# The high half of the first MoE's gated product moves to ScalarE, and the low half of its last two groups to VectorE

## The chip, the cores and the metric

The kernel runs on one core of one Trainium2 chip. The metric is the device time of one execution in microseconds (us): the median of several runs. A profile of one execution shows every engine: TensorE (PE, with its weight loads as PEld), VectorE (DVE), ScalarE (ACT), GpSimd (POOL) and the queue of SyncE that issues the DMAs (SP).

## The reference

Three stages are chained: an attention with a decaying mask, a first MoE layer with a maximum of three products, and a second one with a rational function. Shapes: 4 batches of 576 tokens, 8 heads of 64, so 2304 tokens by 512; 768 and 2048 hidden columns.

```python
scores = scale * q @ k.T + decay            # causal, decay from cumsum(log(clip(f)))
attn = softmax(scores);  x = attn @ v       # 2304 x 512

h = np.maximum(np.maximum(x @ w1, x @ w2), x @ w3)     # 2304 x 768
x = h @ w_out                                          # 2304 x 512

h = x @ w_in                                           # 2304 x 2048
P = a[0] + a[1]*h + a[2]*h*h + a[3]*h*h*h
Q = 1.0 + abs(b[0])*abs(h) + abs(b[1])*h*h
out = (P / (Q + 1e-6)) @ w_out2                        # 2304 x 512
```

The weights arrive as 64-bit floats, which the kernel converts itself.

## The kernel before

**Numbers in two parts.** Matmul operands are float32r. A value is written as a high part (the value rounded to float32r by a copy) and a low part (the value less the high one), and each product is three matmuls: high by high, high by low, low by high.

**Groups and units.** Tokens go in groups (batch b, part g): g = 0 has 320 columns, g = 1 has 256, so there are eight groups. For each group the first MoE has 18 units `moe1_h` (six column blocks fc, three matrices j) and then four units `moe1_o` (dc).

- `moe1_h` (lines 422 to 442) makes 12 matmuls into one PSUM bank (lines 429 to 431). For j = 0 ScalarE copies the bank into an SBUF tile `m` (line 434); for j = 1 and 2 VectorE takes the maximum of that and the next bank (line 436). After j = 2 the gated product is split into the tile `hh`: its high part on line 440 (GpSimd multiplies by one), its low part on line 441 (GpSimd subtracts).
- `moe1_o` (lines 444 to 459) runs over all six `hh` of the group: three matmuls for each fc, on lines 453 and 454 (by the high part) and 455 (by the low part), into `x2p`. ScalarE and VectorE split the result into `xo` (lines 457 and 458), and a DMA takes it to DRAM.

**What runs beside it.** The units are put between the steps of the attention. Its normalisation of `e` (line 360) and copies of keys and queries (lines 267 and 281) are on GpSimd, its exponentials (line 350) and copies of transposed weights `pt` (line 385) on ScalarE. The last two groups (b = 3) are left over and come after the attention: from there `tail["n"]` is a number and no longer None, `hbank` hands out banks of three pools, and the units stand between 32 conversions of the second MoE's input weights (`convert_wi`, which calls `convert`, lines 151 to 170). One conversion is: a load, ScalarE's absolute value (line 160), VectorE's four operations 161, 162, 163 and 166 on 128 x 256 values, ScalarE's copy to the high part `wih` (line 169), GpSimd's subtraction to the low part `wil` (line 170). Three tiles `cv_wi` go round.

**Who sets the order.** Each engine works through its own queue in order. The order in a queue is not that of the code: a scheduler takes the recorded operations and lays them out by an estimate of its own of when each can run. So a changed operation moves others. Only the second MoE from its second tile on (`manual_schedule`) stands as written.

Of the kernel before, what the change touches and what calls it, by code (L numbers as in the profile page):

```python
# [11 lines left out]
AF = mybir.ActivationFunctionType  # L12
ALU = mybir.AluOpType
# [21 lines left out]
def kernel(  # L35
    ctx: ExitStack, tc: tile.TileContext, q, k, v, f, w1, w2, w3, w_out, m2_in, m2_out, m2_a, m2_b, out
):
    nc = tc.nc
# [11 lines left out]
    def r32(ap):  # L50
        return ap.bitcast(F32)
# [361 lines left out]
    tail = {"n": None}  # L413

    def hbank(name):
        pool, tag = ps_h, "h"
        if tail["n"] is not None:
            pool, tag = TAILP[tail["n"] % len(TAILP)]
            tail["n"] += 1
        return pool.tile([P, 512], F32, name=name, tag=tag)  # L420

    def moe1_h(b, g, fc, j):
        w = GQ[g][1] - GQ[g][0]
        nm_ = f"{b}_{g}_{fc}"
        xs = [xt[b, dc, g] for dc in range(NDC)]
        wh, wl = w1t[fc]
        hp_ = hbank(f"h{j}_{nm_}")
        for dc in reversed(range(NDC)):
            nc.tensor.matmul(hp_[:, :w], wh[:, j, dc], xs[dc][:, 1], start=(dc == NDC - 1), stop=False)  # L429
            nc.tensor.matmul(hp_[:, :w], wh[:, j, dc], xs[dc][:, 0], start=False, stop=False)  # L430
            nc.tensor.matmul(hp_[:, :w], wl[:, j, dc], xs[dc][:, 0], start=False, stop=(dc == 0))  # L431
        nxt = mpool.tile([P, 320], F32, name=f"m{j}_{nm_}", tag="mx", bufs=3)
        if j == 0:
            nc.scalar.activation(nxt[:, :w], hp_[:, :w], AF.Copy)
        else:
            nc.vector.tensor_tensor(nxt[:, :w], cur[0][:, :w], hp_[:, :w], op=ALU.max)  # L436
        cur[0] = nxt
        if j == 2:
            hh = mpool.tile([P, 2, 320], F32R, name=f"hh_{nm_}", tag="hh", bufs=6)
            nc.gpsimd.tensor_scalar(hh[:, 0, :w], nxt[:, :w], 1.0, 0.0, op0=ALU.mult, op1=ALU.add)  # L440
            nc.gpsimd.tensor_tensor(hh[:, 1, :w], nxt[:, :w], r32(hh[:, 0, :w]), op=ALU.subtract)
            hs[b, g, fc] = hh

    def moe1_o(b, g, dc):
# [16 lines left out]
    def moe1_units(b, g):  # L461
        return [lambda fc=fc, j=j: moe1_h(b, g, fc, j) for fc in range(NF1) for j in range(3)] + [
            lambda dc=dc: moe1_o(b, g, dc) for dc in range(NDC)
        ]
# [72 lines left out]
    for step in range(len(slots) + 2):  # L537
# [4 lines left out]
        if u is not None and u.pair.n + 1 < len(pairs):  # L542
            n = u.pair.n + 1
# [252 lines left out]
```

## Time and profile before

| | |
|---|---|
| median of 3 runs | 1014.16 us (1014.15 to 1014.49) |
| the profiled execution's own time | 1014.65 us |
| its span, first to last instruction | 1012.8 us |
| TensorE busy | 984.6 us, 97% of the span |
| VectorE, ScalarE, GpSimd busy | 74%, 61%, 28% |
| mean granted TensorE clock | 0.989 |

The span is 1.85 us shorter than the profiled execution's time, and that time is 0.49 us over the median. The attention with the first six groups lasts to about 520 us, the last two groups of the first MoE from there to 607.5 us, the second MoE to the end. The busy time of TensorE includes the ends of pipelined matmuls, which are modelled: a matmul of 320 columns is shown as 0.31 us, while the next one starts 0.15 us after it. A granted clock of 1.00 is 2.4 GHz, of 0.50 it is 1.2 GHz; a value between is a stretch with both.

### The profile page before, as it was taken

What the parts mean: (1) busy time and instruction counts of PE and PEld (TensorE: products, weight loads), DVE (VectorE), ACT (ScalarE), POOL (GpSimd) and SP (SyncE); (2) the same over time, 40 slices, a digit from 0 to 9 for tenths busy, and PEclk for the clock granted to TensorE, in tenths of its full rate; (3) what the DMA queues carried; (4) which work ended last, traced back from release to release, by engine and by line L of the source; (5) the groups of instructions that cost most, each with busy time, mean ns of one, the idle gap of its engine ahead of it and who ended that gap; (6) DMA issues with size and microseconds to landing.
All of it is one profiled execution on the core that took longest, in us unless ns stands there. A gap on an engine that the chain in (4) does not pass through costs nothing.

```text
span 1012.8 us, 16900 instructions
## 1 busy us (share of the span) xinstructions
PE 984.6 (97%) x5780; PEld 831.2 (82%) x5780; DVE 750.6 (74%) x1744; ACT 613.5 (61%) x1409; POOL 286.7 (28%) x498
## 2 busy tenths in 40 slices
PE   8989999999999999999998989999999999999998
PEld 5657778887888888988898987888888888899997
DVE  4779984555677676644349676988988888899997
ACT  4775665656655566554434336766766666677775
POOL 1545763543554554443326440000000000000000
PEclk9998999999999999999999999999999999999999
DMA  4574223213444355221034529301001100200000
GB/s 122 162 213 132 79 57 89 47 41 104 119 128 151 104 154 179 81 59 48 1 116 146 177 80 344 128 1 49 35 1 63 42 1 1 95 10 1 32 1 32
DMA packets 118453, 86.69 MB, mean 86 GB/s; under 512 B 67280, under 2 KB 103136, under 8 KB 118368
## 3 DMA queue, kind: packets, MB, share of 16 engines
q1 hardware_dynamic: 118368, 85.62, 27.9%
q8 instruction: 46, 0.75, 0.3%
q14 instruction: 39, 0.32, 0.1%
HBM read 62.90 MB, written 22.69 MB: 85 GB/s over the span
## 4 chain that ended last, share of the span: by engine, by line
PE 77%; DVE 14%; issue 3%; DMA 3%; ACT 2%; POOL 1%; SPq 0%; DVEq 0%; POOLq 0%; ACTq 0%
PE oo L719 7%; PE oo L720 7%; PE oo L718 6%; PE o L399 6%; PE hq L669 6%; PE hq L671 6%; PE hq L670 6%; PE tp L381 5%; PE h L429 5%; PE h L430 4%; PE h L431 4%; PE s L342 2%; PE x2p L453 2%; PE x2p L455 2%; PE x2p L454 2%
## 5 line engine op out<-in xcount | busy, mean ns | idle before, releaser
L429 PE MATMUL h<-x,w1h 128*128 128x320 f32 (+1 forms) x576 | 176.9, 307 | 2.1 <-DVE m L436 2.0
L430 PE MATMUL h<-x,w1h 128*128 128x320 f32 (+1 forms) x576 | 173.0, 300 | 0.0
L431 PE MATMUL h<-x,w1l 128*128 128x320 f32 (+1 forms) x576 | 172.7, 300 | 0.0
L360 POOL TENSOR_SCALAR e<-e,rs 64x64 f32<-64x64 f32 (+4 forms) x160 | 88.6, 565 | 114.5 <-DVE rs L356 87.9
L350 ACT ACTIVATE e<-e,st 64x64 f32<-64x64 f32 (+4 forms) x160 | 89.3, 558 | 51.7 <-DVE st L344 48.9
L429 PEld LDWEIGHTS h<-x,w1h 128*128 128x128 f32 x576 | 110.3, 192 | 8.8 <-DVE m L436 3.7
L719 PE MATMUL oo<-wp,gh 128*128 128x512 f32 x288 | 112.8, 392 | 0.0
L718 PE MATMUL oo<-wp,gh 128*128 128x512 f32 x288 | 112.4, 390 | 0.0
L430 PEld LDWEIGHTS h<-x,w1h 128*128 128x128 f32 x576 | 110.2, 191 | 2.2 <-issue 2.0
L344 DVE CUSTOM_DVE_ANT_0 e<-s,mask 128x320 f32<-128x320 f32 (+3 forms) x160 | 68.1, 432 | 57.6 <-PE s L343 37.3
L431 PEld LDWEIGHTS h<-x,w1l 128*128 128x128 f32 x576 | 110.0, 191 | 0.1
L720 PE MATMUL oo<-wp,gl 128*128 128x512 f32 x288 | 108.8, 392 | 0.0
L678 ACT ACTIVATE s<-hq 128x512 f32<-128x512 f32 (+1 forms) x80 | 44.3, 554 | 97.2 <-PE hq L671 97.1
L385 ACT ACTIVATE pt<-tp 128x384 f32<-128x384 f32 (+3 forms) x160 | 69.8, 471 | 31.6 <-PE tp L381 28.7
L399 PE MATMUL o<-pt,v 128*64 128x256 f32 (+3 forms) x512 | 83.0, 371 | 0.3 <-ACT pt L385 0.3
L381 PE MATMUL tp<-ident,e 128*128 128x128 f32 (+2 forms) x480 | 81.4, 278 | 0.6 <-POOL e L360 0.5
L681 DVE SCALAR_TENSOR_TENSOR s<-s,ab,u 128x512 f32<-128x512 f32 (+1 forms) x80 | 55.8, 698 | 31.8 <-ACT u L679 31.6
L671 PE MATMUL hq<-x,wil 128*128 128x512 f32 (+1 forms) x192 | 70.4, 366 | 0.0
L669 PE MATMUL hq<-x,wih 128*128 128x512 f32 (+1 forms) x192 | 70.4, 366 | 0.0
L670 PE MATMUL hq<-x,wih 128*128 128x512 f32 (+1 forms) x192 | 70.3, 366 | 0.0
L453 PE MATMUL x2p<-hh,wo 128*128 128x320 f32 (+1 forms) x192 | 59.6, 314 | 7.2 <-POOL hh L440 5.9
L381 PEld LDWEIGHTS tp<-ident,e 128*128 128x128 f32 (+2 forms) x480 | 54.3, 132 | 13.6 <-issue 7.0
(128 smaller groups left out, 2444.6 us busy)
## 6 DMA issues: line engine op xcount, KB each, us to landing
raw_w<-in_moe_w_dram SPq DMA_DIRECT2D x18, 512.0 KB
raw_wp<-in_moe_w_out_dram SPq DMA_DIRECT2D x32, 256.0 KB
wpd<-wp SPq DMA_DIRECT2D x32, 256.0 KB
raw_wi<-in_moe_w_in_dram SPq DMA_DIRECT2D x32, 256.0 KB
wp<-wpd SPq DMA_DIRECT2D x10, 768.0 KB
x2d<-xo SPq DMA_DIRECT2D x16, 320.0 KB
out_dram<-ob SPq DMA_DIRECT2D x18, 256.0 KB
kn<-in_k_dram SPq DMA_DIRECT2D x32, 128.0 KB
```

Source lines behind the costliest of these rows:

```text
L350: nc.scalar.activation(e[:nr], e[:nr], AF.Exp, bias=m, scale=-1.0, accum_out=l)
L381: nc.tensor.transpose(tp[:kr, dst : dst + nr], self.e[i][:nr, Q0[c] : Q1[c]], ident[:nr, :nr])
L399: nc.tensor.matmul(ot[SIDES[i][0], q0 - lo : w], p.v[:kr, c, i], p.pt[g][:kr, i, col : col + hi - q0], start=(j == 0), stop=(j == len(orde ...
L429: nc.tensor.matmul(hp_[:, :w], wh[:, j, dc], xs[dc][:, 1], start=(dc == NDC - 1), stop=False)
L430: nc.tensor.matmul(hp_[:, :w], wh[:, j, dc], xs[dc][:, 0], start=False, stop=False)
L431: nc.tensor.matmul(hp_[:, :w], wl[:, j, dc], xs[dc][:, 0], start=False, stop=(dc == 0))
L669: nc.tensor.matmul(hp_[:, :w], wih[:, dc, fs], xh, start=(dc == 0), stop=False)
L670: nc.tensor.matmul(hp_[:, :w], wih[:, dc, fs], xl, start=False, stop=False)
L671: nc.tensor.matmul(hp_[:, :w], wil[:, dc, fs], xh, start=False, stop=(dc == NDC - 1))
L718: nc.tensor.matmul(o, g[0][:, ts_], wh_, start=(fc == 0), stop=False)
L719: nc.tensor.matmul(o, g[0][:, ts_], wl_, start=False, stop=False)
L720: nc.tensor.matmul(o, g[1][:, ts_], wh_, start=False, stop=(fc == NF2 - 1))
```

## The change

The high part of `hh` is written by ScalarE as a copy, in all 48 places. The low part stays on GpSimd in the 36 that are recorded during the attention, and goes to VectorE in the 12 of the last two groups. Nothing else is edited; from line 441 on the changed kernel's line numbers are one higher, so its low part is line 442 and the split of `xo` lines 458 and 459.

```diff
         if j == 2:
             hh = mpool.tile([P, 2, 320], F32R, name=f"hh_{nm_}", tag="hh", bufs=6)
-            nc.gpsimd.tensor_scalar(hh[:, 0, :w], nxt[:, :w], 1.0, 0.0, op0=ALU.mult, op1=ALU.add)
-            nc.gpsimd.tensor_tensor(hh[:, 1, :w], nxt[:, :w], r32(hh[:, 0, :w]), op=ALU.subtract)
+            nc.scalar.activation(hh[:, 0, :w], nxt[:, :w], AF.Copy)
+            eng = nc.gpsimd if tail["n"] is None else nc.vector
+            eng.tensor_tensor(hh[:, 1, :w], nxt[:, :w], r32(hh[:, 0, :w]), op=ALU.subtract)
             hs[b, g, fc] = hh
```

The scheduler lays the queues out anew. In the rows below a name such as `hh_3_0_4` is the tile of batch 3, part 0, block fc 4; `m1` and `m2` are the maxima after j = 1 and j = 2; `cv_wi_2_7` is the tile of one conversion.

**VectorE, the last two groups, around block 4 of group (3, 0).** Before:

```order
L161 TENSOR_SCALAR cv_wi_2_7_7317<-cv_wi_2_7_7317 128x256
L166 SCALAR_TENSOR_TENSOR cv_wi_0_7_7284<-raw_wi_0_7_7201,cv_wi_0_7_7284 128x256
L162 TENSOR_SCALAR cv_wi_2_7_7317<-cv_wi_2_7_7317 128x256
L161 TENSOR_SCALAR cv_wi_0_8_7327<-cv_wi_0_8_7327 128x256
L436 TENSOR_TENSOR m2_3_0_4_7116<-m1_3_0_4_7081,h2_3_0_4_7103 128x320
L163 SCALAR_TENSOR_TENSOR cv_wi_2_7_7317<-raw_wi_2_7_7229,cv_wi_2_7_7317 128x256
L162 TENSOR_SCALAR cv_wi_0_8_7327<-cv_wi_0_8_7327 128x256
L166 SCALAR_TENSOR_TENSOR cv_wi_2_7_7317<-raw_wi_2_7_7229,cv_wi_2_7_7317 128x256
L163 SCALAR_TENSOR_TENSOR cv_wi_0_8_7327<-raw_wi_0_8_7239,cv_wi_0_8_7327 128x256
L166 SCALAR_TENSOR_TENSOR cv_wi_0_8_7327<-raw_wi_0_8_7239,cv_wi_0_8_7327 128x256
L436 TENSOR_TENSOR m1_3_0_5_7189<-m0_3_0_5_7154,h1_3_0_5_7176 128x320
L436 TENSOR_TENSOR m2_3_0_5_7224<-m1_3_0_5_7189,h2_3_0_5_7211 128x320
```

And of the change:

```order
L161 TENSOR_SCALAR cv_wi_2_7_7317<-cv_wi_2_7_7317 128x256
L166 SCALAR_TENSOR_TENSOR cv_wi_0_7_7284<-raw_wi_0_7_7201,cv_wi_0_7_7284 128x256
L436 TENSOR_TENSOR m2_3_0_4_7116<-m1_3_0_4_7081,h2_3_0_4_7103 128x320
L162 TENSOR_SCALAR cv_wi_2_7_7317<-cv_wi_2_7_7317 128x256
L161 TENSOR_SCALAR cv_wi_0_8_7327<-cv_wi_0_8_7327 128x256
L163 SCALAR_TENSOR_TENSOR cv_wi_2_7_7317<-raw_wi_2_7_7229,cv_wi_2_7_7317 128x256
L162 TENSOR_SCALAR cv_wi_0_8_7327<-cv_wi_0_8_7327 128x256
L442 TENSOR_TENSOR hh_3_0_4_7118<-m2_3_0_4_7116,hh_3_0_4_7118 128x320
L166 SCALAR_TENSOR_TENSOR cv_wi_2_7_7317<-raw_wi_2_7_7229,cv_wi_2_7_7317 128x256
L163 SCALAR_TENSOR_TENSOR cv_wi_0_8_7327<-raw_wi_0_8_7239,cv_wi_0_8_7327 128x256
L166 SCALAR_TENSOR_TENSOR cv_wi_0_8_7327<-raw_wi_0_8_7239,cv_wi_0_8_7327 128x256
L436 TENSOR_TENSOR m1_3_0_5_7189<-m0_3_0_5_7154,h1_3_0_5_7176 128x320
```

The maximum `m2_3_0_4` stands two conversion operations earlier, and the low part of `hh_3_0_4` four operations behind it. Block 4 of group (3, 1) has the same pattern, with its maximum one operation (an L166) earlier and its low part two operations behind it. Each of the other ten blocks has one L442 more in this queue.

**ScalarE at the same place.** Before:

```order
L160 ACTIVATE cv_wi_0_8_7327<-raw_wi_0_8_7239 128x256
L169 ACTIVATE wih_7013<-cv_wi_0_7_7284 128x2x128
L434 ACTIVATE m0_3_0_5_7154<-h0_3_0_5_7141 128x320
L169 ACTIVATE wih_7013<-cv_wi_2_7_7317 128x2x128
L169 ACTIVATE wih_7013<-cv_wi_0_8_7327 128x2x128
```

And of the change:

```order
L160 ACTIVATE cv_wi_0_8_7327<-raw_wi_0_8_7239 128x256
L169 ACTIVATE wih_7013<-cv_wi_0_7_7284 128x2x128
L440 ACTIVATE hh_3_0_4_7118<-m2_3_0_4_7116 128x320
L434 ACTIVATE m0_3_0_5_7154<-h0_3_0_5_7141 128x320
L169 ACTIVATE wih_7013<-cv_wi_2_7_7317 128x2x128
L169 ACTIVATE wih_7013<-cv_wi_0_8_7327 128x2x128
L440 ACTIVATE hh_3_0_5_7226<-m2_3_0_5_7224 128x320
```

What stands ahead of the high part, the copy `wih` of `cv_wi_0_7`, waits for an L166 that is ahead of `m2_3_0_4` on VectorE too.

**ScalarE during the attention, around block 3 of group (2, 0), of the change.**

```order
L385 ACTIVATE pt_16_0_1_5426<-tp1_16_1_1_5546 128x384
L385 ACTIVATE pt_16_0_1_5426<-tp2_16_1_1_5551 64x256
L169 ACTIVATE wp_15_1_5641<-cv_wp_15_1_5642 128x256
L440 ACTIVATE hh_2_0_3_5666<-m2_2_0_3_5664 128x320
L350 ACTIVATE e1_17_1_0_5683,rs_17_1_0_5675<-e1_17_1_0_5683,st_17_1_0_5674 128x192
L350 ACTIVATE e2_17_1_0_5689,rs_17_1_0_5675<-e2_17_1_0_5689,st_17_1_0_5674 128x320
```

Here the high part, which waits for a maximum of VectorE, stands ahead of two exponentials; before, GpSimd had it, between a conversion (L170) and the low part, with three normalisations (L360) behind.

## Rows read from the trace of the kernel before

**Rows 1.** The page, busy time of each engine over the span.
```profile
PE 984.6 (97%) x5780; PEld 831.2 (82%) x5780; DVE 750.6 (74%) x1744; ACT 613.5 (61%) x1409; POOL 286.7 (28%) x498
```
**Rows 2.** Stretches: start:end, length, busy us of each engine, granted clock, DMA share, GB/s.
```profile
557.30:561.00 3.70, 3.70 (x17) 3.70 (x17) 1.72 (x3) 0.42 (x1) 2.57 (x4) 0.55 0.00 0
...
598.60:602.10 3.50, 3.24 (x15) 2.94 (x15) 0.73 (x2) 0.42 (x1) 2.35 (x4) 0.51 0.00 0
...
625.00:1012.80 387.80, 383.79 (x1756) 324.69 (x1754) 342.07 (x557) 266.43 (x475) 0.00 (x0) 1.00 0.11 40
```
**Rows 3.** Timeline of TensorE, 553 to 557.4 us: start, duration, line; in brackets, idle before.
```profile
553.30 0.31 PE L455 MATMUL x2p<-hh,wo 128*128 128x320 f32 x1
555.83 0.41 PE L453 MATMUL x2p<-hh,wo 128*128 128x320 f32 x1 [2.22 <-POOL hh L440]
...
557.02 0.42 PE L455 MATMUL x2p<-hh,wo 128*128 128x320 f32 x1 [0.64 <-POOL hh L441]
```
**Rows 4.** Timeline of TensorE, 594 to 599.5 us.
```profile
594.41 0.28 PE L455 MATMUL x2p<-hh,wo 128*128 128x256 f32 x1
598.37 0.39 PE L453 MATMUL x2p<-hh,wo 128*128 128x256 f32 x1 [3.67 <-POOL hh L440]
...
599.22 0.58 PE L455 MATMUL x2p<-hh,wo 128*128 128x256 f32 x1 [0.26 <-POOL hh L441]
```
**Rows 5.** Timeline of VectorE, 551.6 to 559 us.
```profile
553.51 0.41 DVE L166 SCALAR_TENSOR_TENSOR cv_wi<-raw_wi,cv_wi 128x256 int32<-128x256 int32 x1
553.85 0.28 DVE L162 TENSOR_SCALAR cv_wi<-cv_wi 128x256 int32<-128x256 int32 x1
554.05 0.28 DVE L161 TENSOR_SCALAR cv_wi<-cv_wi 128x256 f32<-128x256 f32 x1
554.25 0.47 DVE L436 TENSOR_TENSOR m<-m,h 128x320 f32<-128x320 f32 x1
```
**Rows 6.** Timeline of VectorE, 594 to 600 us.
```profile
596.96 0.41 DVE L436 TENSOR_TENSOR m<-m,h 128x256 f32<-128x256 f32 x1
```
**Rows 7.** Groups by shape, VectorE, 524.3 to 554.7 us: busy, mean ns | idle before.
```profile
L163 DVE SCALAR_TENSOR_TENSOR cv_wi<-raw_wi,cv_wi 128x256 int32<-128x256 int32 x15 | 9.8, 651 | 0.1
L166 DVE SCALAR_TENSOR_TENSOR cv_wi<-raw_wi,cv_wi 128x256 int32<-128x256 int32 x15 | 8.9, 594 | 0.1
L161 DVE TENSOR_SCALAR cv_wi<-cv_wi 128x256 f32<-128x256 f32 x15 | 6.5, 431 | 0.8 <-ACT cv_wi L160 0.8
L162 DVE TENSOR_SCALAR cv_wi<-cv_wi 128x256 int32<-128x256 int32 x14 | 5.4, 389 | 0.1
L436 DVE TENSOR_TENSOR m<-m,h 128x320 f32<-128x320 f32 x10 | 4.8, 477 | 0.0
```
**Rows 8.** Groups by shape, GpSimd, 524.3 to 554.7 us.
```profile
L170 POOL TENSOR_TENSOR wil<-cv_wi,wih 128x256 fp32r<-128x256 f32 x15 | 12.3, 822 | 25.3 <-ACT wih L169 25.3
L441 POOL TENSOR_TENSOR hh<-m,hh 128x320 fp32r<-128x320 f32 x4 | 3.7, 916 | 0.3
L440 POOL TENSOR_SCALAR hh<-m 128x320 fp32r<-128x320 f32 x4 | 2.2, 539 | 2.1 <-DVE m L436 2.1
```
**Rows 9.** Groups by shape, GpSimd, 570.9 to 597.4 us.
```profile
L441 POOL TENSOR_TENSOR hh<-m,hh 128x256 fp32r<-128x256 f32 x4 | 3.5, 872 | 0.2
L440 POOL TENSOR_SCALAR hh<-m 128x256 fp32r<-128x256 f32 x4 | 2.1, 520 | 3.4 <-DVE m L436 3.4
```
**Rows 10.** Groups by shape, VectorE, 625 to 1012 us (GpSimd does nothing there).
```profile
L702 DVE TENSOR_TENSOR gl<-t,gh 128x384 fp32r<-128x384 f32 x32 | 17.7, 552 | 0.7 <-ACT gh L698 0.7
```
**Rows 11.** Groups, ScalarE, 76 to 520 us.
```profile
L434 ACT ACTIVATE m<-h 128x320 f32<-128x320 f32 (+1 forms) x36 | 14.4, 401 | 8.6 <-PE h L431 5.0 <-PE s L343 2.4 <-PE s L342 1.0
```
**Rows 12.** Waits, 76 to 520 us: engine, line and its releaser, us in total, times, longest.
```profile
POOL hh L440 <- DVE m L436: 24.0, 13, 3.9
...
PE x2p L454 <- POOL wo L170: 1.2, 1, 1.2
...
PE o L399 <- ACT pt L385: 0.3, 1, 0.3
```

## The prediction

> **What bounds the kernel now.** I read the busy shares first, then stretches of time, then the timelines at the places where TensorE stands still. TensorE is the busiest engine, at 97% [rows 1]; to the end, from 625 us, it is busy 383.8 of 387.8 us [rows 2], with no GpSimd work there. So whatever is saved earlier arrives whole at the end, and an engine that is not TensorE counts only where TensorE waits for it. The places where it waits for what the change touches are two. In the last two groups of the first MoE, the block fc 4 is late both times: TensorE starts an L455 at 553.30 us and the next matmul only at 555.83, after 2.22 us of idleness that ended with GpSimd's high part, and then waits 0.64 us for the low part [rows 3]. In the second group it goes from 594.41 to 598.37, with 0.26 us more for the low part [rows 4]. As matmuls of these forms otherwise start 0.15 and 0.12 us apart, the high parts cost 2.38 and 3.84 us, and the two places 7.1 us together. Behind each the granted clock is low: 0.55 for 3.7 us and 0.51 for 3.5 us [rows 2], which is 2.4 GHz for part of them and 1.2 GHz for the rest, and costs 3.7 x 0.45 = 1.7 and 3.5 x 0.49 = 1.7 us. In all 10.5 us, 1% of the run, hang on these twelve blocks.
>
> GpSimd is only the last link there. The maximum that it splits begins on VectorE at 554.25 us [rows 5] and 596.96 us [rows 6], when TensorE already waits. VectorE is late because it stands in a queue without gaps [rows 7], and its operations are stretched. One conversion operation takes 0.41 us (L166; L163 has the same form) or 0.28 us (L161, L162) where GpSimd is idle [rows 5], but 0.65, 0.59, 0.43 and 0.39 us in the mean over 30 us before the first stall, while the maxima, with one operand in PSUM, keep their 0.47 to 0.48 us [rows 5, 7]. The stretch is 15 x 0.24 + 15 x 0.18 + 15 x 0.15 + 14 x 0.11 = 10.1 us, beside 12.3 + 3.7 + 2.2 = 18.2 us of GpSimd [rows 8]: 0.56 us of VectorE lost for each us in which GpSimd works.
>
> **The change part by part, first of the two groups.**
>
> *Removed from GpSimd:* before the late maximum, the splits of blocks 0 to 3, 3.7 + 2.2 = 5.9 us [rows 8]. At 0.56 this gives VectorE back 3.3 us.
>
> *Added to VectorE:* four low parts of 320 columns, both operands in SBUF. No row has one; between 0.41 us for 256 columns [rows 5] and 0.55 for 384 [rows 10] it is 0.48, of which the queue feels 0.41, since the next starts about 0.07 us before an operation's end (553.51 to 553.85). If they are stretched as L163 is (0.65 against 0.41) they cost 0.65. So 1.6 to 2.6 us; I take 2.1, since two of three conversion conflicts remain with L170.
>
> *Moved:* two conversion operations stand behind the maximum now, at 0.20 us of the queue each [rows 5]: 0.4 us. The maximum thus starts 3.3 - 2.1 + 0.4 = 1.6 us earlier, at 552.65 and ends at 553.12.
>
> *High part on ScalarE:* its copies of this size take 0.40 us [rows 11]; with 0.05 us of handing over it is there at 553.57. What stands ahead of it in ScalarE's queue waits for the same VectorE rows, so nothing holds it longer. TensorE wants it at 553.45: 0.1 us of waiting. *Low part on VectorE:* behind the maximum (0.40) come four operations, 0.94 us free, 1.2 with conflicts; the low part begins at 554.25 and ends at about 554.85. TensorE has then waited from 553.86: 1.0 us. Block 5 follows after an L166, an L163, an L166 and two maxima, 2.2 us, and its copy; TensorE needs 14 matmuls of 0.15 for that, 2.1, and waits some 0.5. In place of 3.0 us it waits 1.6, in three pieces, and I take the low clock for gone: 1.4 + 1.7 = **3.1 us**.
>
> The Trainium skill weighs against this part. Its page "SBUF — State Buffer" (section "Practical consequences") says that a VectorE instruction with two SBUF inputs contends with a GpSimd instruction that reads SBUF, that the one that comes second is blocked until the other's end, and that one SBUF input alone is free of it. The stretched conversions and the untouched maxima agree [rows 5, 7]. By that rule a low part meets an L170 in 12.3 of 30.4 us and then loses up to its 0.82 us, 0.33 us in the mean, so that four cost 3.0 us in place of 2.1: 0.9 us less in each group, 1010.2 us in all. The sum here goes by the rows.
>
> **Second group.** Blocks 0 to 3 take 3.5 + 2.1 = 5.6 us of GpSimd [rows 9]: 3.1 us back. Four low parts of 256 columns take 0.35 of the queue free, 0.56 stretched: 1.4 to 2.2, taken at 1.8. One L166 is moved behind the maximum, 0.34. It starts 1.6 us earlier, at 595.32, the high part is there at 596.18 in place of 598.37, the low part, two operations later, at 597.05, which TensorE waits 0.6 for in place of 0.26. That is 2.2 - 0.35 = 1.85 us. A wait of 1.65 us is left, and I count half of the low clock: **2.7 us**. VectorE's work of this group begins when TensorE ends that of the first, so the two gains add up.
>
> **Attention.** 36 high parts go from GpSimd to ScalarE, 36 x 0.40 = 14.4 us [rows 11], and the scheduler lays the queues out anew. TensorE waited for ScalarE's `pt` only 0.3 us there, and 1.2 us for a GpSimd subtraction [rows 12]; both engines have room, ScalarE being busy 61% [rows 1]. I put it at nothing. Ends: a gain of 1.2 us and one low clock, 2.9 us; a loss of a quarter of the copies' time, 3.6 us, if some stand in the way of exponentials. At the GpSimd end nothing is late next: its queue had the two instructions and has one.
>
> **Sum.** 3.1 + 2.7 = 5.8 us. The profiled execution took 1014.65 us, its span 1012.8; less 5.8 that is 1008.85, and as the median is 0.49 us under the profiled execution, **1008.4 us**. The terms' ends give 1003 to 1012.
>
> **Rivals.**
>
> *The low parts are blocked whole (slower).* Each low part meets an L170 and stands still for all of its 0.82 us [rows 8]. Four cost 4 x 1.23 = 4.9 us against 3.3 + 0.4 given back: the maximum comes 1.2 us later, the high part 0.5 us, the low part 1.1 us. In the second group 4.7 against 3.4: 1.3 us later, the low part 1.2. Both low clocks stay: 1.1 + 1.2 = 2.3 us lost, **1016.5 us**. It is the rule of the skill's page above at its hardest. It decides from 0.93 us a low part on. For it: all conversions have GpSimd work beside them. Against it: GpSimd is idle 25.3 us before L170 in the first stretch [rows 8]. Chance 0.14.
>
> *ScalarE blocks the attention.* GpSimd stood 24.0 us before the high part in 13 waits for VectorE's maxima [rows 12]. Now ScalarE stands there, with exponentials behind it. If a third of that, 8 us, reaches TensorE, the sum is 2.2 us slower: **1016.4 us**. Against it: GpSimd had the normalisations behind the same wait, and TensorE waited for none of it. Chance 0.12.
>
> *All of it goes.* VectorE catches up by more, both stalls and both low clocks vanish, 10.5 us, and the attention gives up to 2.9: **1000.8 to 1003.7 us**. Against it: the low part still stands behind two to four conversions. Chance 0.12.
>
> That the change doesn't do what it says is excluded by the order: twelve L442 stand on VectorE, all in the last two groups.
>
> **How the numbers follow.** The forecast has 0.62. A measurement of this kernel can tell about 0.2%, 2 us: faster is below 1012.1, slower above 1016.2. Faster: most of the forecast and the last rival, 0.72. The two slow rivals lie at the bound: 0.14 slower, 0.14 within it. The range takes in half of the slow rivals' way and most of the last: 1002.0 to 1014.5.
>
> **What would show it.** Right: the waits of TensorE at L453 for the high part shrink to under 2 us in all and name ScalarE; the conversions' means in the last two groups fall; the low clock after the first is gone; from 625 us on nothing differs. Wrong: L442 takes over 0.9 us in the mean; TensorE waits as long for VectorE; or the last attention matmul comes more than 3 us later or earlier than before.

## The result and the profile after

The changed kernel takes 1002.1 us (median of 4 runs, 1001.8 to 1003.0) against 1014.33 (4 runs, 1014.15 to 1015.82): a ratio of 0.988, 95% interval 0.9865 to 0.9895, or 12.2 us. The forecast of 1008.4 had the sign and the mechanism, and less than half of the size. What came lies inside the rival "all of it goes" (1000.8 to 1003.7), though not by its way: part of the waits stayed. The profiled execution took 1003.0 us, its span 1001.2.

The page, busy time of each engine, answers to [rows 1]:

```profile
PE 982.4 (98%) x5780; PEld 826.6 (83%) x5780; DVE 747.5 (75%) x1756; ACT 631.3 (63%) x1457; POOL 255.9 (26%) x438
```

GpSimd has lost 30.8 us of work and ScalarE gained 17.8, and TensorE is the busiest engine as before, at 98%. The gain lies where TensorE stood still. Stretches of the changed kernel, columns as in [rows 2]: the one behind the first stall of before, the last matmuls (L454 to L456) of either group, and the rest.

```profile
557.30:561.00 3.70, 3.70 (x29) 3.70 (x28) 1.78 (x6) 1.30 (x3) 0.00 (x0) 1.00 0.99 300
548.80:560.40 11.60, 11.23 (x75) 10.70 (x75) 6.79 (x18) 4.55 (x11) 2.44 (x3) 1.00 0.59 189
586.20:597.00 10.80, 9.41 (x75) 8.80 (x74) 6.51 (x17) 3.32 (x9) 2.29 (x3) 1.00 0.20 62
614.40:1001.20 386.80, 383.18 (x1754) 324.19 (x1752) 341.48 (x556) 265.88 (x474) 0.00 (x0) 1.00 0.11 40
```

The granted clock is 1.00 in all of them, where before had 0.55 and 0.51 behind its stalls [rows 2]: both low clocks are gone. The long last stretch is 1.0 us shorter than its counterpart of before, 387.8 [rows 2], but holds two matmuls fewer. From the matmul behind the only long wait of TensorE in the second MoE (622.77 us before, 611.58 after) to the last one (1008.40 and 997.19) TensorE is 11.2 us earlier throughout, so the middle of that stretch did not change; the last 0.4 us lie behind the last matmul.

The timeline of TensorE, at the places of [rows 3, 4]:

```profile
548.76 0.31 PE L454 MATMUL x2p<-hh,wo 128*128 128x320 f32 x1
...
550.67 0.31 PE L455 MATMUL x2p<-hh,wo 128*128 128x320 f32 x1
551.05 0.42 PE L456 MATMUL x2p<-hh,wo 128*128 128x320 f32 x1
...
553.67 0.42 PE L454 MATMUL x2p<-hh,wo 128*128 128x320 f32 x1 [0.30 <-ACT hh L440]
...
586.16 0.28 PE L454 MATMUL x2p<-hh,wo 128*128 128x256 f32 x1
...
588.97 0.38 PE L454 MATMUL x2p<-hh,wo 128*128 128x256 f32 x1 [1.21 <-ACT hh L440]
```

and the first matmuls of the same groups before, line 453 there:

```profile
551.69 0.31 PE L453 MATMUL x2p<-hh,wo 128*128 128x320 f32 x1
...
593.09 0.28 PE L453 MATMUL x2p<-hh,wo 128*128 128x256 f32 x1
```

In the first of the two groups block 4 costs no wait for its high part, and 0.23 us where it wants the low part (the L456 at 551.05, in place of 0.15 us behind 550.67); block 5 costs 0.30. In the second the wait for block 4 is 1.21 us in place of 3.67. The releaser is ScalarE, as the change has it, but the reason is on VectorE, whose timeline stands beside [rows 5, 6]:

```profile
548.63 0.47 DVE L436 TENSOR_TENSOR m<-m,h 128x320 f32<-128x320 f32 x1
...
549.44 0.96 DVE L163 SCALAR_TENSOR_TENSOR cv_wi<-raw_wi,cv_wi 128x256 int32<-128x256 int32 x1
550.32 0.28 DVE L162 TENSOR_SCALAR cv_wi<-cv_wi 128x256 int32<-128x256 int32 x1
550.52 0.48 DVE L442 TENSOR_TENSOR hh<-m,hh 128x320 fp32r<-128x320 f32 x1
...
588.05 0.41 DVE L436 TENSOR_TENSOR m<-m,h 128x256 f32<-128x256 f32 x1
```

Counted from the group's first matmul, the maximum of block 4 starts 0.13 us ahead in the first group, in place of 2.56 behind, and in the second 1.89 behind in place of 3.87. Of the low part's lateness 0.55 us is one conversion, the L163 at 549.44 that took 0.96 instead of 0.41. The high part follows its maximum closely on ScalarE:

```profile
549.14 0.47 ACT L440 ACTIVATE hh<-m 128x320 fp32r<-128x320 f32 x1
...
588.50 0.42 ACT L440 ACTIVATE hh<-m 128x256 fp32r<-128x256 f32 x1 [1.40 <-DVE m L436]
```

Groups of VectorE and GpSimd by shape, 521.4 to 549.1 us, beside [rows 7, 8]:

```profile
L166 DVE SCALAR_TENSOR_TENSOR cv_wi<-raw_wi,cv_wi 128x256 int32<-128x256 int32 x15 | 7.3, 489 | 0.0
L163 DVE SCALAR_TENSOR_TENSOR cv_wi<-raw_wi,cv_wi 128x256 int32<-128x256 int32 x14 | 6.8, 485 | 0.1
L162 DVE TENSOR_SCALAR cv_wi<-cv_wi 128x256 int32<-128x256 int32 x14 | 6.1, 434 | 0.1
L436 DVE TENSOR_TENSOR m<-m,h 128x320 f32<-128x320 f32 x10 | 4.7, 474 | 0.0
L161 DVE TENSOR_SCALAR cv_wi<-cv_wi 128x256 f32<-128x256 f32 x13 | 4.2, 326 | 1.2 <-ACT cv_wi L160 1.1
L442 DVE TENSOR_TENSOR hh<-m,hh 128x320 fp32r<-128x320 f32 x4 | 2.5, 616 | 0.0
...
L170 POOL TENSOR_TENSOR wil<-cv_wi,wih 128x256 fp32r<-128x256 f32 x14 | 12.2, 878 | 29.1 <-ACT wih L169 29.1
```

L163 and L166 fall from 651 and 594 ns to 485 and 489, L161 from 431 to 326; L162 rises from 389 to 434. L170 is still there with its 12.2 us. Low parts now stand among the conversions.

Where the 11.6 us of the span went, by the ends of stretches in the two timelines:

| | before | after | gain |
|---|---|---|---|
| last matmul of the attention ends | 519.29 | 516.37 | 2.9 |
| last matmuls of group (3, 0), length | 15.65 | 11.65 | 4.0 |
| last matmuls of group (3, 1), length | 14.57 | 10.97 | 3.6 |
| from there to the end | 405.18 | 404.09 | 1.1 |

### The profile page after: what moved, and what is told of

Same layout as the page of the kernel before. It is cut to its first block, busy times and chain, and to the rows that moved or that the text cites. A ratio compares the mean times of both kernels' runs of the same rounds, so it can differ in the third digit from the quotient of the medians.

```text
span 1001.2 us, 16877 instructions
## 1 busy us (share of the span) xinstructions
PE 982.4 (98%) x5780; PEld 826.6 (83%) x5780; DVE 747.5 (75%) x1756; ACT 631.3 (63%) x1457; POOL 255.9 (26%) x438
## 4 chain that ended last, share of the span: by engine, by line
PE 80%; DVE 11%; DMA 4%; issue 2%; ACT 2%; SPq 1%; POOL 0%; DVEq 0%; ACTq 0%
PE o L399 7%; PE oo L720 7%; PE oo L721 7%; PE oo L719 7%; PE hq L670 6%; PE hq L672 6%; PE hq L671 6%; PE h L429 5%; PE tp L381 5%; PE h L430 5%; PE h L431 5%; PE s L342 2%; PE s L343 2%; PE x2p L454 2%; PE x2p L456 2%
## 5 line engine op out<-in xcount | busy, mean ns | idle before, releaser
L360 POOL TENSOR_SCALAR e<-e,rs 64x64 f32<-64x64 f32 (+4 forms) x160 | 88.7, 567 | 117.3 <-DVE rs L356 87.5
L385 ACT ACTIVATE pt<-tp 128x384 f32<-128x384 f32 (+3 forms) x160 | 69.8, 470 | 31.2 <-PE tp L381 30.2
L399 PEld LDWEIGHTS o<-pt,v 128*64 128x64 f32 (+1 forms) x512 | 37.0, 135 | 35.5 <-issue 21.0
```

The lines of the kernel that those rows point to most:

```text
L399: nc.tensor.matmul(ot[SIDES[i][0], q0 - lo : w], p.v[:kr, c, i], p.pt[g][:kr, i, col : col + hi - q0], start=(j == 0), stop=(j == len(orde ...
```

## The experiments

Two theories were set against each other. **A**: GpSimd's two instructions a block slowed VectorE's conversions, so the maximum came late; the change helps by taking work off GpSimd beside VectorE. **B**: GpSimd was a slow last link, two instructions one behind the other; the change helps by a shorter chain behind the maximum. The profiled execution of every run is condensed here, from its timeline: the end of the attention's last matmul, the length of the two groups' last matmuls, and the start of block 4's maximum against the group's first of them, in us.

| | median, ratio to before [95%] | attention | (3, 0) | (3, 1) | maximum |
|---|---|---|---|---|---|
| before | | 519.29 | 15.65 | 14.57 | +2.56, +3.87 |
| the change | 1002.1, 0.988 [0.9865, 0.9895] | 516.37 | 11.65 | 10.97 | -0.13, +1.89 |
| low_gpsimd | 1007.05, 0.9914 [0.9887, 0.9942] | 516.42 | 12.14 | 13.20 | +0.42, +3.03 |
| high_gpsimd | 1010.35, 0.9945 [0.9928, 0.9963] | 523.17 | 13.44 | 12.82 | -0.04, +0.83 |
| last_two_only | 1006.34, 0.9901 [0.9884, 0.9919] | 520.47 | 11.47 | 10.20 | -0.28, +1.14 |
| attention_only | 1012.43, 0.9953 [0.9937, 0.997] | 516.74 | 15.51 | 15.67 | +2.54, +3.75 |
| ghost_both | 1010.44, 0.9961 [0.9945, 0.9977] | 517.73 | 15.78 | 13.57 | +2.94, +2.91 |
| ghost_multiply | 1004.7, 0.9898 [0.987, 0.9926] | 516.38 | 12.00 | 11.86 | -0.04, +2.46 |
| ghost_subtract | 1007.22, 0.9918 [0.9891, 0.9945] | 516.16 | 14.36 | 12.28 | +1.21, +1.82 |
| no_gpsimd_last | 1000.3, 0.9852 [0.9822, 0.9883] | 516.54 | 10.72 | 8.80 | -4.98, -4.08 |
| only_l170_moved | 1006.0, 0.99 [0.9872, 0.9929] | 520.25 | 11.04 | 9.33 | -2.48, -1.91 |

The first four edits, from low_gpsimd to attention_only, ran on one chip (before: 1016.45 us), the next four on another (1014.18), the rest on a third (1016.28). Ratios are to the kernel before on the same chip. The expectations were written for a kernel before of 1014.3 us, so on the first and third chip a time stands some 2 us high beside them.

**One half of the change at a time.** low_gpsimd leaves the low part on GpSimd everywhere (diffs are against the changed kernel):

```diff
-            eng = nc.gpsimd if tail["n"] is None else nc.vector
-            eng.tensor_tensor(hh[:, 1, :w], nxt[:, :w], r32(hh[:, 0, :w]), op=ALU.subtract)
+            nc.gpsimd.tensor_tensor(hh[:, 1, :w], nxt[:, :w], r32(hh[:, 0, :w]), op=ALU.subtract)
```

> High part on ScalarE in all 48 places, low part on GpSimd in all 48: the second half of the change is undone. Theory A (in the last two groups VectorE's maximum is late because GpSimd's work stretches VectorE's conversion operations; whatever leaves GpSimd brings the maximum forward): the four high parts that leave GpSimd before the late maximum free 2.2 us of it, 1.2 us of VectorE, and VectorE is spared four low parts of some 0.41 us; so the maximum comes about as early as in the change, only the low part is later by a GpSimd subtraction (0.87 us, perhaps behind an L170 of 0.82): 1002 to 1005 us. Theory B (what counted was that high and low part stood behind GpSimd's conversions in its queue; VectorE's lateness is not touched): the low part is still there, so more than half of the gain of the two groups is lost: 1006 to 1010 us.

high_gpsimd leaves the high part on GpSimd, with the low part as changed:

```diff
-            nc.scalar.activation(hh[:, 0, :w], nxt[:, :w], AF.Copy)
+            nc.gpsimd.tensor_scalar(hh[:, 0, :w], nxt[:, :w], 1.0, 0.0, op0=ALU.mult, op1=ALU.add)
```

> High part on GpSimd in all 48 places as before, low part on VectorE in the last two groups: the first half of the change is undone. Theory A: the low parts that leave GpSimd give VectorE back 2.1 us before the late maximum and cost it about as much; the maximum comes at most 0.5 us earlier, the high part still takes 0.54 us on GpSimd behind an L170: 1010 to 1014 us. Theory B: half of the queue is gone, so about half of the gain in the last two groups (3 to 4 us): 1009 to 1011 us. If the attention's 2.9 us came from the high parts there, they are gone in both.

Measured: 1007.05 us for the first and 1010.35 for the second. The second's profiled execution, 1014.82 us, is the slowest of its ten, with long low clocks in the attention, so its two groups are read and not its span. In the two groups the halves save 4.9 and 4.0 us, 8.8 together, and the change 7.6: each half brings about half. Each keeps one low clock, in the second group, of 1.7 us. The waits of TensorE show why (us in total, times, longest). For low_gpsimd:

```profile
PE x2p L453 <- ACT hh L440: 2.9, 2, 2.3
```

and for high_gpsimd:

```profile
PE x2p L454 <- POOL hh L440: 2.1, 2, 1.4
PE x2p L456 <- DVE hh L442: 2.1, 2, 1.3
```

With the low part left on GpSimd, the high part on ScalarE is as late as its maximum, which in the second group comes 3.03 us behind the first matmul. With the low part on VectorE the maximum is early in both groups, but the high part then stands in GpSimd's queue and the low part behind it. So the prompt last link has its share (B). The times don't decide between the two: 1007.05 lies in B's range, but by its ratio, some 1005.6 on the first chip, between the two ranges, and 1010.35 lies in both, by its ratio (some 1008.8) below both. On the maximum of high_gpsimd A was wrong as written: it came 2.6 and 3.0 us earlier, not at most 0.5. A needs a test that leaves the link alone.

**One place at a time.** last_two_only applies the change in the last two groups alone, attention_only in the attention alone:

```diff
-            nc.scalar.activation(hh[:, 0, :w], nxt[:, :w], AF.Copy)
-            eng = nc.gpsimd if tail["n"] is None else nc.vector
-            eng.tensor_tensor(hh[:, 1, :w], nxt[:, :w], r32(hh[:, 0, :w]), op=ALU.subtract)
+            if tail["n"] is None:
+                nc.gpsimd.tensor_scalar(hh[:, 0, :w], nxt[:, :w], 1.0, 0.0, op0=ALU.mult, op1=ALU.add)
+                nc.gpsimd.tensor_tensor(hh[:, 1, :w], nxt[:, :w], r32(hh[:, 0, :w]), op=ALU.subtract)
+            else:
+                nc.scalar.activation(hh[:, 0, :w], nxt[:, :w], AF.Copy)
+                nc.vector.tensor_tensor(hh[:, 1, :w], nxt[:, :w], r32(hh[:, 0, :w]), op=ALU.subtract)
```

> The change in the last two groups alone: during the attention both parts are on GpSimd as before. The last attention matmul ended 2.9 us earlier with the change. If that came from the high parts on ScalarE (theory C), it is back at 519 us and the time is 1004.5 to 1006 us. If it is chance of the new layout of the queues (theory D), the end of the attention falls anywhere between 513 and 522 us; the stretch from there to the end keeps its gain of 8.7 us in both.

> The change in the attention alone: 36 high parts on ScalarE, the last two groups as before. Theory C: the attention ends near 516.4 us and the rest is as before: 1010.5 to 1012 us. Theory D: the end of the attention lies anywhere between 513 and 522 us, and the waits of TensorE for the two blocks fc 4 are as before (over 6 us together) with a low clock behind each.

Measured: 1006.34 and 1012.43 us. The first saves 8.5 us in the two groups and nothing in the attention; the second ends the attention at 516.74, as early as the change, and has both stalls and both low clocks of before in the last groups. So the attention's gain goes with its high parts, and the two places are separate gains. In the traces they add up; by the medians on this chip they are 10.1 and 4.0 us, more than the change's 12.2, with intervals of nearly 2 us to either side.

**GpSimd's work put back, off the chain.** ghost_both is the changed kernel with GpSimd multiplying and subtracting again in the last two groups, from the same maximum, but into the attention's mask tile, which nothing reads any more:

```diff
+            if tail["n"] is not None:
+                nc.gpsimd.tensor_scalar(mask[:, :w], nxt[:, :w], 1.0, 0.0, op0=ALU.mult, op1=ALU.add)
+                nc.gpsimd.tensor_tensor(mask[:, :w], nxt[:, :w], mask[:, :w], op=ALU.subtract)
```

> The change, and in the last two groups GpSimd also does what it did before, a multiplication by one and a subtraction of the same maximum, into a tile that nobody reads any more (the mask of the attention). Nothing waits for these results. Theory A (GpSimd's work beside VectorE's conversions is what makes the maximum late): the late maximum starts 2.5 us or more after the first of the x2p matmuls in the first group and 3.5 us or more in the second, as before the change, and of the 8.7 us that the last two groups and what follows gained at least 5 are lost: 1007 to 1012 us. Theory B (only the place in GpSimd's queue counted): the maximum stays as early as with the change, 1002 to 1004 us.

Measured: 1010.44 us. The maxima are back at +2.94 and +2.91, and of the 7.6 us that the change won in the two groups 6.7 are lost, though in these groups TensorE waits for nothing that GpSimd writes. The second maximum falls short of the 3.5 us that A had written, and 3.4 of the 6.7 us are the two low clocks, which are back. Its timeline:

```profile
554.11 0.42 PE L457 MATMUL x2p<-hh,wo 128*128 128x320 f32 x1 [2.06 <-ACT hh L440]
...
555.80 0.64 PE L459 MATMUL x2p<-hh,wo 128*128 128x320 f32 x1 [1.13 <-DVE hh L442]
...
595.48 0.39 PE L457 MATMUL x2p<-hh,wo 128*128 128x256 f32 x1 [2.23 <-ACT hh L440]
```

and those of VectorE and GpSimd at the low part that ends the second of these waits:

```profile
554.60 1.14 DVE L442 TENSOR_TENSOR hh<-m,hh 128x320 fp32r<-128x320 f32 x1
...
554.29 1.11 POOL L445 TENSOR_TENSOR mask<-m,mask 128x320 f32<-128x320 f32 x1
```

The low part, free at 0.48, begins 0.31 us behind the ghost's subtraction and ends 0.34 behind it. The queues were laid out anew here too, but that is not what made the maximum late: as many conversion instructions stand ahead of it as in the change (61 and 53, against 60 and 54), nothing waits for the ghost's two instructions, and VectorE is idle less (0.7 and 0.5 us, against 1.7 and 1.3). What grew is the time that the conversions and four low parts take up to it: 28.2 and 24.8 us, against 23.8 and 22.8. This is theory A shown: the same chain, late again, by GpSimd's work beside VectorE alone. Which of the two instructions is dear, the next two runs tell; each keeps one of them (the subtraction there takes the maximum twice).

> The same with the multiplication alone, 0.45 to 0.54 us each. Theory A with a price by time (0.56 to 0.6 us of VectorE for a us of GpSimd): 2.2 us before the late maximum, so it comes about 1.2 us later than with the change: 1003 to 1006 us. Theory A2 (the subtraction with two inputs does the harm, the multiplication little: the kernel with the high parts left on GpSimd had its maximum as early as the change): within 1 us of the change.

> The same with the subtraction alone, 0.87 us each. Theory A by time: 3.6 us of GpSimd before the late maximum, 2.1 us later: 1004 to 1008 us. Theory A2: nearly all of what both together cost: within 1.5 us of that kernel. Theory B: as the change, 1002 to 1004 us.

Measured: 1004.7 and 1007.22 us. In the two groups the multiplication alone costs 1.2 us, the subtraction 4.0, both together 6.7. Neither has a low clock in these groups. The one that went to VectorE was the dear one. Both forms of A were wrong in part: the price does not go by GpSimd's time (the subtraction lasts 0.75 us in the middle, the multiplication 0.48), and the subtraction alone is 3.2 us faster than both, not within 1.5.

**L170 taken off GpSimd too.** no_gpsimd_last is the change with the low part of the weights' conversion on VectorE in the last two groups, where GpSimd then does nothing:

```diff
-        nc.gpsimd.tensor_tensor(lo, tf, r32(hi), op=ALU.subtract)
+        eng = nc.gpsimd if tail["n"] is None else nc.vector
+        eng.tensor_tensor(lo, tf, r32(hi), op=ALU.subtract)
```

> The change, and in the last two groups VectorE also makes the conversions' low parts (line 170), so that GpSimd does nothing there. Theory A: 26 us of GpSimd leave, at 0.6 some 15 us of VectorE; 32 subtractions of 256 columns cost it 32 x 0.35 = 11 us. Every conversion operation takes its free 0.28 or 0.41 us in the mean, the late maxima come no later than with the change, and at most the 1.3 us of waiting that are left in the second group go: 1000.5 to 1003 us. Theory B: VectorE gets 11 us more and nothing back, the maxima come 4 to 5 us later in each group: 1008 us or more.

Measured: 1000.3 us (999.71 to 1000.51), the lowest median of all. By the ratios a gain over the change is not shown, since the intervals overlap; in the traces the two groups are 3.1 us shorter. Its stretches of last matmuls:

```profile
548.93:559.65 10.72, 10.72 (x76) 10.72 (x75) 5.45 (x16) 3.59 (x9) 0.00 (x0) 1.00 0.57 187
585.41:594.21 8.80, 8.80 (x74) 8.60 (x72) 4.85 (x15) 2.84 (x8) 0.00 (x0) 1.00 0.21 61
```

TensorE is busy throughout, so these lengths are what the two groups cost without any wait. VectorE has more to do and is earlier: the maximum comes 4.98 us before TensorE's first matmul. A page of the Trainium skill, "Perfetto Trace Analysis" (section "Optimizing Scalar/DVE Operations"), says that because the two share a read port of SBUF, moving work between GpSimd and VectorE might not help. Here it helped, from GpSimd to VectorE, as the next run shows by itself: there, up to block 4's maximum of group (3, 0), 56 conversion instructions with twelve of the subtractions took VectorE 21.9 us, where 62 without them took 27.1 before.

The counterpart leaves `hh` wholly on GpSimd, as before, and moves L170 alone:

> The kernel before, with one thing changed: in the last two groups the conversions' low parts (line 170) are VectorE's, and both parts of the gated product stay on GpSimd in all 48 places. Theory A (GpSimd's work beside VectorE's conversions makes the maximum late): 26 us of GpSimd leave in place of the change's 16, so the maximum comes early though nothing of the gated product was moved, TensorE's two waits shrink to under 2 us together, no low clock follows them, and the attention is as before with its two low clocks: 1003.5 to 1006.5 us. Theory B (high and low part are late in GpSimd's queue): they no longer stand behind L170, but VectorE has 11 us more: 1010 us or more.

Measured: 1006.0 us. Its stretches of last matmuls, beside those of no_gpsimd_last:

```profile
552.64:563.68 11.04, 11.04 (x76) 10.72 (x75) 6.77 (x16) 2.93 (x8) 2.38 (x3) 1.00 0.55 179
589.43:598.76 9.33, 9.07 (x74) 8.66 (x72) 5.85 (x18) 2.74 (x7) 1.88 (x3) 1.00 0.22 63
```

All but 0.9 us of the waits is gone with GpSimd still the last link, two instructions long. B alone cannot do that. The link still matters where the maximum is not early enough to cover it: in high_gpsimd it came at -0.04 and +0.83, and the two groups were 6.7 us over those of no_gpsimd_last.

**The attention.** Where the 2.9 us come from, stretches of both kernels show. Before:

```profile
145.00:153.00 8.00, 6.79 (x33) 5.51 (x34) 5.21 (x15) 5.63 (x17) 6.84 (x13) 0.79 0.28 64
244.00:252.00 8.00, 6.56 (x35) 6.13 (x34) 7.19 (x25) 5.56 (x16) 4.00 (x9) 0.79 0.26 57
```

and after:

```profile
145.00:153.00 8.00, 7.11 (x46) 5.77 (x45) 4.91 (x14) 5.05 (x15) 5.87 (x12) 1.00 0.33 75
244.00:252.00 8.00, 7.75 (x56) 7.59 (x57) 5.22 (x22) 5.68 (x19) 4.27 (x9) 1.00 0.63 181
```

Two more low clocks, 8 x 0.21 = 1.7 us each, have gone. With the two waits ahead of them that is more than the 2.9 us of the balance; what took the rest back was not followed. All four layouts with the attention's high parts on GpSimd (before, high_gpsimd, last_two_only, only_l170_moved) have both, with a granted clock of 0.71 to 0.79 there; of the eight with all of them on ScalarE only ghost_both has one there. The timeline of TensorE before shows a wait ahead of each, and ahead of these a longer one, at 102 us, with a granted clock of 1.00 behind it:

```profile
102.22 0.41 PE L429 MATMUL h<-x,w1h 128*128 128x320 f32 x1 [1.47 <-DVE m L436]
...
147.82 0.44 PE L454 MATMUL x2p<-hh,wo 128*128 128x320 f32 x1 [1.21 <-POOL wo L170]
...
245.21 0.21 PE L342 MATMUL s<-k1s,q1s 128*64 128x64 f32 x1 [0.96 <-DVE q1s L278]
```

The change has neither of the last two. To find which of the attention's groups does it, last_two_only was given ScalarE's high parts in group (0, 0) alone, or in (0, 1) and (1, 0) alone:

```diff
-            nc.scalar.activation(hh[:, 0, :w], nxt[:, :w], AF.Copy)
-            eng = nc.gpsimd if tail["n"] is None else nc.vector
-            eng.tensor_tensor(hh[:, 1, :w], nxt[:, :w], r32(hh[:, 0, :w]), op=ALU.subtract)
+            if tail["n"] is not None or (b, g) == (0, 0):
+                nc.scalar.activation(hh[:, 0, :w], nxt[:, :w], AF.Copy)
+                (nc.gpsimd if tail["n"] is None else nc.vector).tensor_tensor(hh[:, 1, :w], nxt[:, :w], r32(hh[:, 0, :w]), op=ALU.subtract)
+            else:
+                nc.gpsimd.tensor_scalar(hh[:, 0, :w], nxt[:, :w], 1.0, 0.0, op0=ALU.mult, op1=ALU.add)
+                nc.gpsimd.tensor_tensor(hh[:, 1, :w], nxt[:, :w], r32(hh[:, 0, :w]), op=ALU.subtract)
```

> The change in the last two groups, and in the attention high parts on ScalarE in the first group (0, 0) alone. The kernels with high parts on GpSimd in the attention had low clocks at 148 and at 247 us in the profile (three of three), those with them on ScalarE none in six of seven, one at 149 us in the seventh. Theory C (each low clock hangs on the wait that stands ahead of it, and the moved high parts shorten that wait): the wait of 1.2 us for GpSimd's L170 at 148 us goes and its low clock with it, the one at 247 us stays: the attention ends about 1.5 us earlier than in the kernel with the last two groups alone, 518.5 to 519.5 us. Theory D (layout): anywhere else.

> The change in the last two groups, and in the attention high parts on ScalarE in groups (0, 1) and (1, 0) alone. Theory C: the wait at 148 us and its low clock stay, the wait of 1 us for VectorE's line 278 at 246 us goes and the low clock at 247 us with it; the attention ends at 518.5 to 519.5 us. Theory D: anywhere else.

Measured: 1005.19 and 1008.0 us. The first ended its attention at 518.70, within what was written, but by another way: the wait at 147.8 and both low clocks are gone, and a new wait, 377.26 us for ScalarE's `pt`, 1.46 us long, has a low clock behind it, 0.79 in 375 to 383 us. The wait for line 278 stays there too, 0.98 us at 244.4, without a low clock. The second ended its attention at 520.08, later than was written and only 0.4 us earlier than in last_two_only; it keeps the wait for L170 and the first low clock and loses the second one, while the wait ahead of that stays, at the same 0.96 us:

```profile
247.34 0.21 PE L342 MATMUL s<-k1s,q1s 128*64 128x64 f32 x1 [0.96 <-DVE q1s L278]
```

So the first wait of 1.21 us is bound to group (0, 0) alone: a `wo` subtraction of GpSimd comes late where the same queue has the high parts. That a low clock hangs on the wait ahead of it, as theory C has it, is not borne out: equal waits went both ways, and what decides it stays open. Nor is a low clock less worth its 1.7 us at the attention's end: the second run has a new wait of 1.02 us for ScalarE's `pt`, at 316.3.

A last run asked whether the attention's 36 low parts should go to VectorE as well, on top of no_gpsimd_last:

```diff
-            eng = nc.gpsimd if tail["n"] is None else nc.vector
-            eng.tensor_tensor(hh[:, 1, :w], nxt[:, :w], r32(hh[:, 0, :w]), op=ALU.subtract)
+            nc.vector.tensor_tensor(hh[:, 1, :w], nxt[:, :w], r32(hh[:, 0, :w]), op=ALU.subtract)
```

> The fastest kernel so far (change, and L170 of the last two groups on VectorE) with the low parts of the attention's 36 blocks on VectorE too. VectorE is busy some 64% there and GpSimd 45%. If GpSimd's work costs VectorE time in the attention as well, VectorE gains 36 x 0.86 x 0.6 = 18 us and pays 36 x 0.38 = 14 us, which TensorE hardly sees: 998 to 1002 us. If VectorE's queue holds back the scores' minima (line 344), TensorE waits for it: 1003 us or more.

Measured: 1002.87 us (1002.33 to 1005.99), ratio 0.9869, interval 0.9846 to 0.9892: no gain over no_gpsimd_last. A wait of 1.67 us for VectorE's `st` at 376.81 us is new, with a low clock behind it (0.79 in 375 to 383).

## Why the prediction was right or wrong

**What bounds the kernel: right.** TensorE's standstills at block 4 and the low clocks behind them were the price, and the maximum's lateness on VectorE the cause; ghost_both and only_l170_moved show that. The 10.5 us put on the two places stand beside 10.7 (30.2 in before less 19.5 in no_gpsimd_last).

**First group: 3.1 forecast, 4.0 measured.** The step that failed is "at 0.56 this gives VectorE back 3.3 us". Summing VectorE's rows from start to next start, from the end of the previous group's matmuls to block 4's maximum:

| group (3, 0) | before | after |
|---|---|---|
| conversions (62, 60 instructions) | 27.1 | 21.7 |
| four low parts | 0 | 2.2 |
| maxima and the split of `xo` | 3.9 | 4.0 |
| idle | 1.2 | 1.7 |
| | 32.6 | 29.9 |

(The first 0.45 us of each stretch, the end of an instruction under way and a short wait, is in the totals alone.) The conversions give back 5.4 us. Two fewer stand ahead, 0.4 as forecast; the other 5.0, put down to the 5.9 us of GpSimd's work removed, are 0.85 for each us. The 0.56 was a mean over all of GpSimd's work, most of it L170 that stays, and in this group what was taken away cost more than the mean. The price of the low parts, 2.1, was right at 2.2 although they went unlike either end: three at 0.48 free, one at 1.03. So the maximum came 2.7 us earlier, not 1.6, and of the 1.6 us of waiting that was to stay 0.9 stayed (11.65 against 10.72). The low clock went, as forecast.

**Second group: 2.7 forecast, 3.6 measured.** Here the relief was not larger: conversions fell from 25.2 to 21.5 us with four fewer ahead (1.1 us free), so 2.6 against the 3.1 forecast, 0.46 for each of the 5.6 us removed. Why the price differs so between the groups stays open. But the four low parts cost 1.3 instead of 1.8, all free at 0.41, and three more conversion instructions were already done when the group began, since VectorE had caught up in the first. The maximum came 2.0 us earlier, not 1.6, the wait fell to 1.21, and the low clock, counted by half, went whole: 0.85 us of the 0.9 missing.

**The low parts' blocking.** The weighing of the rule on the Trainium skill's page "SBUF — State Buffer" (section "Who interferes with whom") had 3.0 us for four of them. The durations are indeed of two kinds, free or blocked for most of an L170, as the Trainium skill says there; but one of twelve met an L170, not the share of time that L170 fills. The rival that had them blocked whole did not come about. The prediction has one SBUF input alone free of contention; the Trainium skill says so there only outside the modes in which VectorE uses both of its port pairs. L161 and L162 have one input and were stretched, to 0.43 and 0.39 us from 0.28 [rows 5, 7]; in which mode they ran no run shows.

**The attention: 0 forecast, 2.9 measured**, at the very end named for it. The step that failed is "I put it at nothing": a wait of 1.2 us and a low clock were seen as the upper end and given no weight. The runs show two low clocks lost with the high parts' move, and two waits of 1.21 and 0.96 us ahead of them. That the sum of one wait and one low clock, 2.9, is the very number is chance.

**From there to the end: 0 forecast, 1.1 measured.** One wait of the second MoE for VectorE fell from 0.75 to 0.45 us, and 0.4 us lie behind the last matmul. From 623 us of before to that matmul nothing changed, as the prediction had it from 625 us on.

Together 1.8 + 2.9 + 1.1 = 5.8 us, the whole difference of the spans, 11.6 against 5.8. The other 0.5 us of the medians: the profiled execution after lies 0.9 us above its median, where 0.49 was reckoned. That 1002.1 still lies in the stated range, 0.1 us from its end, is luck: 4.0 us of the gain come from places that the sum had put at nothing.

## What to carry to other kernels

When an engine waits for a last link, look one step further back, at what runs beside the engine that feeds it and stretches its instructions: here each part of GpSimd's work that was taken from beside VectorE's conversions in the last two groups helped, even work that VectorE then had to do itself. Price removed contention by the instructions that are removed (put them back into a dead tile to measure it), not by the mean of all that contend. And count the low clock behind a wait of TensorE as a cost that can go with it: the two in the last groups were 3.4 of the 7.6 us won there.

## What the runs showed of the hardware that was not expected

GpSimd's instructions are stretched too, by VectorE's. In only_l170_moved its groups by shape, 525.3 to 550 us, beside [rows 8], where the same two took 539 and 916 ns:

```profile
L441 POOL TENSOR_SCALAR hh<-m 128x320 fp32r<-128x320 f32 x4 | 5.4, 1344 | 25.2 <-DVE m L437 25.2
L442 POOL TENSOR_TENSOR hh<-m,hh 128x320 fp32r<-128x320 f32 x4 | 4.8, 1189 | 0.3
```

One multiplication took 2.58 us:

```profile
539.40 2.58 POOL L441 TENSOR_SCALAR hh<-m 128x320 fp32r<-128x320 f32 x1 [3.45 <-DVE m L437]
```

Nine of VectorE's instructions begin in that time, one behind the other, and all keep their free durations of 0.28, 0.41 to 0.42 or 0.48 us. That the order of issue decides who stands still is what the Trainium skill says on the page "SBUF — State Buffer" (section "Who interferes with whom"). The trace agrees in that one side alone stands still; it does so over nine instructions here, not only to the end of one.

Waits of TensorE and low clocks do not go by length alone: 1.47 us at 102 us before had a granted clock of 1.00 behind it, and 1.21 us at 147.8 one of 0.79 over 8 us; after, 1.21 us at 588.97 had 1.00.
